# A row tile turned through DRAM is scaled and split one attention stage later, and the attention stream starts two slots sooner

## The chip, the cores and the metric

One core of one Trainium2 chip runs the whole program. TensorE (PE) does the matrix products and has a row of its own for loading weights (PEld); VectorE (DVE), ScalarE (ACT) and GpSimd (POOL) do the element-wise work; SyncE (SP) issues nearly all DMA transfers. The metric is device microseconds (us) from one launch, lower is better.

## What is computed

Three layers follow each other, in float32.

```python
# 1. gated linear attention: B 4, H 8, S 768, D 48
for t in range(S):
    state = alpha[:, :, t, :, None] * state + einsum('bhd,bhe->bhde', k[:, :, t], v[:, :, t])
    y[:, :, t] = einsum('bhd,bhde->bhe', q[:, :, t], state)
x = y.transpose(0, 2, 1, 3).reshape(B * S, H * D)      # 3072 tokens x 384
# 2. RMS norm and gated feed-forward layer, 384 -> 1536 -> 384
xn = x / sqrt(mean(x * x, -1) + 1e-6) * rms_g
x = (silu(xn @ w_gate) * (xn @ w_val)) @ w_out
# 3. eight experts, each token goes to the one with the highest logit
out[mask_e] = gate_w * sigmoid(x @ w_output_gate)[e] * (relu(x[mask_e] @ w1[e]) @ w2[e])
```

## The kernel before, in words

The 3,072 tokens are 24 tiles of 128 tokens. Three tiles form a group of 384 tokens, and the feed-forward layer runs over eight groups. A group has 12 chunks j of 128 hidden columns, and each chunk takes three **slots** of TensorE: gate(j) (nine matmuls into ps_g), val(j) (nine into ps_v) and out(j-1) (nine into ps_o, 400 columns). So a group has 36 slots. Each product is split into a high and a low part in a 32-bit form for matmuls (xh and xl for the input, hh and hl for the hidden values), hence the nine matmuls of 3 x 3. Between the slots, ACT makes tt = silu(ps_g) (L647), DVE multiplies it by ps_v (L666), ACT rounds it to hh (L669) and DVE subtracts to give hl (L675). The out slot reads hh and hl.

The attention of later tiles is woven into these slots. Every tile has five **stages** (`moved`, for tiles 9 to 23): scores (s_), a second stage, output and state together (yd_), keys (keys_) and rows (rows_). A stage runs behind the slot whose number satisfies the test in the last lines of the code below, in which `LEADG` says how many slots ahead of the even spread the stream stands. What the names mean:

- ps_y (L467, L471) is the attention output of a tile in PSUM, with P the masked scores (L443), wide a copy of the state for the next tile (L439) and ps_st (L492) the state update.
- ACT squares ps_y and sums it into ss (L477). POOL turns ss into 1/rms in two operations (L478, L479). ACT writes the normalised rows xn (L480). There is one xn buffer.
- `turn_x`, in rows_: DVE turns xn in 32 x 32 blocks into P's space (L512), four DMAs write it to DRAM as mid_x (L517), and one DMA reads it back, transposed, into xn (L518).
- `put_x`: ACT scales xn by rms_g in three pieces (L526), copies it to xh (L527), and DVE subtracts to give xl (L528). xh and xl are the input of a later group.
- `turn_k`, in keys_: DVE turns the keys of the next tile through the buffer Z (L556), four DMAs write mid_k (L561), one reads it back as kn. Z has one buffer. The next tile's scan (L318) writes Z again, behind a memset of one element by POOL (L408), and both have to wait until the mid_k writes have read Z.

The kernel goes through a tile scheduler that orders each engine's instructions by its own estimate of readiness, unless an instruction is held in source order by `keep_in_program_order`. That, and the stage table, set the order around the change.

Of the kernel before, what the change touches and what calls it, by code (L numbers as in the profile page):

```python
# [12 lines left out]
AF = mybir.ActivationFunctionType  # L13
ALU = mybir.AluOpType
# [5 lines left out]
CFG = {  # L20
    'START': 'a0 r0 a1 w6 c q0 k0 k1 r1 q1 w0 s0 s0 a2 y0 s1 r2 c q2 y0 s1 k2 w0 y1 w4 x0 y1 x1 s2 s2 y2 y2 x2 n1 n0 c n2 l l x2 d1 w3 d1 d0 w2 c x0 d2 d2 x1 w1 d0',
    'LOADS': 'a0 q0 a1 k0 q1 k1 a2 v0 w g k2 v1 q2 w v2 w w r w w w w w',
    'SEATS': (3, 5, 4, 6, 1, 1, 0, 5, 0, 2, 4, 4, 5, 0, 3, 2, 6, 1, 4, 4, 4, 2, 2, 1, 6, 3, 0, 6, 6, 4),
# [17 lines left out]
    'TS': 3,  # L41
    'RA': 7,
    'RB': 9,
    'LEADG': 11,
    'NAT': 5,
    'XO': 2,
    'MT': 6,
# [9 lines left out]
def gla_glu_moe_kernel(  # L57
# [16 lines left out]
    nc = tc.nc  # L74
# [5 lines left out]
    NTILE = NT // P  # L80
# [3 lines left out]
    KF = DFF // P  # L84
    E, _, F2 = w1.shape
    KF2 = F2 // P
    GT = 3
# [57 lines left out]
    gT = const.tile([P, KD], F32, name="gT")  # L145
# [30 lines left out]
    def f(x):  # L176
        return x.bitcast(F32)
# [240 lines left out]
    def stages(t):  # L418
# [6 lines left out]
        g, ti = divmod(t, GT)  # L425
# [77 lines left out]
        def group():  # L503
            if ti == 0:
                xT[g] = (act.tile([P, KD, G], F32R, tag="xh", name="xh"),
                         act.tile([P, KD, G], F32R, tag="xl", name="xl"))
# [13 lines left out]
        def put_x():  # L520
            group()
            xh, xl = xT[g]
            xf = Pt["xn"].rearrange("p (a b) -> p a b", a=KD)
            sl = slice(ti * P, ti * P + P)
            for kc in range(KD):
                nc.scalar.activation(xf[:, kc, :], xf[:, kc, :], AF.Copy, scale=gT[:, kc:kc + 1])  # L526
            nc.scalar.activation(xh[:, :, sl], xf, AF.Copy)  # L527
            nc.vector.tensor_tensor(out=xl[:, :, sl], in0=xf, in1=f(xh[:, :, sl]), op=ALU.subtract)  # L528
        moves[t] = (turn_x, put_x)

        def xtr():
# [22 lines left out]
    def turn_k(t):  # L554
        Z, kT = spare[t], pre[t][2]
        nc.vector.transpose(out=flat(Z).rearrange("a (c p d) -> a p c d", c=TW, p=NP),  # L556
                            in_=kT.rearrange("a p (j c) -> a p c j", c=TW))
        mid = dram.tile([P, H * 64], F32, tag="mid_k", name="mid_k", bufs=2)
        dst = mid.rearrange("(j c) (p a d) -> a j (c p) d", c=TW, p=NP, a=TW)
        for a in range(TW):  # L560
            nc.sync.dma_start(dst[a], flat(Z)[32 * a:32 * a + 32].rearrange("j (n d) -> j n d", d=32))  # L561
        kn = att.tile([P, H, 64], F32, tag="kn", name="kn")
        nc.sync.dma_start(flat(kn), mid)
        kq[t] = kn
# [259 lines left out]
    def prep_step():  # L824
        if prep:
            prep.pop(0)()

    def slot(s, n):

        g, j0, _ = runs[s]  # L830
        j, what = j0 + n // 3, n % 3
        if what == 0:
            have(3 * j + 1, 0)
            return m_gate(g, j)
        if what == 1:
            have(3 * j + 2, 0)
            return m_val(g, j)
        m_low(g, j)
        if j > j0:
            have(3 * j, j)  # L840
            m_out(s, j - 1)
        elif s:
            have(3 * runs[s - 1][2], runs[s - 1][2])
            m_out(s - 1, runs[s - 1][2] - 1)
            return lambda: m_evac(s - 1)

    NST = 5
# [65 lines left out]
    laid = []  # L913

    def moved(t):
        s_, k_, y_, d_, _ = stages(t)

        def second():
            if t == DT:
                k_()  # L920
            return laid.pop() if laid else None

        def yd_():
            posts = [y_(), d_()]

            def post():
                for p in posts:
                    if p:
                        p()
            return post  # L930

        def keys_():
            while prep:
                prep_step()
            if t + 1 < NTILE and place_of[t + 1][1] < NCH - 1:
                turn_k(t + 1)

        def rows_():
            moves[t][0]()
            laid.append(moves[t][1])  # L940
        return s_, second, yd_, keys_, rows_

    def rest():
        yield lambda: None
        yield lambda: laid.pop()

# [5 lines left out]
    done = 0  # L952
    GS = GT * NST

    def stage():
        nonlocal done, nprep
        if done % NST == 0:
            while prep:
                prep_step()
            if nprep < NTILE and done != GS - NST:  # L960
                prep.extend(prework(nprep))
                nprep += 1
        done += 1
        return next(att_stream)()
# [50 lines left out]
    def tiny(name, shape, dt=F32):  # L1015
        return xp.tile(shape, dt, name=name)
# [10 lines left out]
    def pick_first():  # L1027
        key = keys()
        km = tiny("km", [P, 1, 1])
        nc.vector.tensor_reduce(out=km, in_=key, op=ALU.max, axis=AX.X)  # L1030
        nc.vector.tensor_tensor(out=lead1, in0=key, in1=km.to_broadcast([P, 1, E]), op=ALU.is_equal)
        nc.vector.tensor_tensor(out=key, in0=lead1, in1=io8, op=ALU.mult)
        nc.vector.tensor_reduce(out=km, in_=key, op=ALU.add, axis=AX.X)
        nc.vector.tensor_tensor(out=adr[:, 0:1, :], in0=kadr, in1=km.to_broadcast([P, 1, 3]), op=ALU.mult)
        addresses(0)
# [23 lines left out]
    def load_w1(p, i):  # L1059
        n = F2 // 4  # L1060
        s = slice(i * n, i * n + n)
        st = act.tile([P, KD, n], F32, tag="stg", name="st1", bufs=4)
        nc.sync.dma_start(st, w1.rearrange("e k n -> (e k) n")[bass.ds(places[p][1], DM), s]
                          .rearrange("(kc p) n -> p kc n", p=P))

        def go():
            w1h, w1l = we[p][0:2]
            for ins in (nc.scalar.activation(w1h[:, :, s], st, AF.Copy),
                        nc.vector.tensor_tensor(out=w1l[:, :, s], in0=st, in1=f(w1h[:, :, s]), op=ALU.subtract)):
                if p == 1 and i < 4:  # L1070
                    tc.keep_in_program_order(ins)
        return go
# [102 lines left out]
    for g in range(2, NG):  # L1175
        last = g == NG - 1
        strict[0] = g + 2 >= CFG['STRICT'] and not last
        if last:
            psA.release()
            att.release()  # L1180
            xp = tc.alloc_tile_pool(name="xp", bufs=1, side="right", reuse_waits="tile")
            psE = tc.alloc_tile_pool(name="psE", bufs=1, space=PSUM)
            psR[:] = [psE, "tr"]
            w1a = [xp.tile([P, KD, F2], F32R, name=f"w1a{i}") for i in range(2)]
            x2[0] = [xp.tile([P, KD, HALF], F32R, name=f"x2a{i}") for i in range(2)]
            we[0] = [*w1a, None, None]
            lead1 = tiny("lead1", [P, 1, E])
            adr = tiny("adr", [P, E, 3], I32)
            er0 = xp.tile([P, 2, RW], F32, name="er0")
            todo = []  # L1190
        for n in range(3 * KF):
            post = slot(g + 2, n)
            if post:
                post()
            if done < (NTILE - GT) * NST + 2 and ((g - 1) * 3 * KF + n + 1 + CFG['LEADG']) * GT >= (done + 1 - GT * NST) * 3 * KF / NST:
                post = stage()
                if post:
                    post()
            prep_step()
            if g == 2 and n in (1, 3):  # L1200
                (route_a, route_b)[n // 2](0)
            if n == CFG['RA']:
                route_a(g - 1)
            if n == CFG['RB']:
                route_b(g - 1)
            if last:
                if n == 9:
                    pick_first()
                if n in (10, 12, 14, 16):
                    todo.append(load_w1(0, (n - 10) // 2))  # L1210
                if n in (18, 20, 22, 24):
                    todo.pop(0)()
                if n == 24:
                    load_rows(0, er0)
                if n >= 28 and n < 28 + 3:
                    prep_rows(0, n - 28)
                if n in (25, 27, 29, 31):
                    todo.append(load_w2(0, (n - 25) // 2))
# [254 lines left out]
```

## Time and profile before

| | |
|---|---|
| median of 3 runs | 863.0 us (862.89 to 867.31) |
| the profiled execution | 866.33 us, span 864.5 us |
| mean granted TensorE clock | 0.990 |
| PE, PEld busy | 835.1 us, 794.0 us |
| DVE, ACT, POOL busy | 513.5, 315.9, 147.3 us |

The span is the time from the first to the last instruction of the core in the profiled execution. That execution is one of its own beside the three timed runs. A busy share is a mean over the whole span. The stretch from about 200 to 550 us is where the turned tiles 9 to 23 pass.

### The profile page before, as it was taken

The page shows a single profiled execution, that of the slowest core. Times are in us where ns is not written, and L with a number is a line of the kernel's source. Part 1 is how long each engine was busy: PE and PEld are TensorE (multiplying, and loading weights), DVE is VectorE, ACT ScalarE, POOL GpSimd, SP SyncE. Part 2 cuts the span into 40 slices and gives each one's busy share as a digit, 9 for nine tenths or more (in the row PEclk, how much of TensorE's full clock was granted, in tenths as well). Part 3 has the DMA queues.
Part 4 walks back from the last instruction along what each step waited for, and adds up shares of the span by engine and source line. Part 5 has one row for each costly group of instructions (what it writes and reads, how often), then busy time and mean ns, then how long its engine had stood idle before and what let it go on. Part 6 is the DMA issues. An engine that isn't in the chain of part 4 may idle for free.

```text
span 864.5 us, 15986 instructions
## 1 busy us (share of the span) xinstructions
PE 835.1 (97%) x6111; PEld 794.0 (92%) x6111; DVE 513.5 (59%) x1136; ACT 315.9 (37%) x695; POOL 147.3 (17%) x204
## 2 busy tenths in 40 slices
PE   7999999999899999999999999999999999999996
PEld 6899999999799889898989989999988999999996
DVE  6899998697667756656666753244453442453331
ACT  1646544332323333322322332234234343453431
POOL 2100000002100010010020010013033243343341
PEclk8999999999999999999999999999999999999999
DMA  9956566755544342244454211032055164266421
GB/s 192 181 156 158 164 138 171 208 140 122 134 96 89 77 117 66 68 106 97 93 130 94 52 38 27 11 98 95 1 192 195 59 215 138 66 201 192 153 69 35
DMA packets 168990, 100.12 MB, mean 116 GB/s; under 512 B 100811, under 2 KB 162764, under 8 KB 168912
## 3 DMA queue, kind: packets, MB, share of 16 engines
q1 hardware_dynamic: 164448, 89.61, 41.7%
q0 software_dynamic: 4464, 9.48, 3.2%
q8 instruction: 48, 0.79, 0.4%
q14 instruction: 30, 0.25, 0.1%
HBM read 77.68 MB, written 21.64 MB: 115 GB/s over the span
## 4 chain that ended last, share of the span: by engine, by line
PE 57%; DMA 14%; DVE 12%; issue 6%; SPq 5%; ACT 4%; POOL 2%; POOLq 0%; DVEq 0%; ACTq 0%
PE ps_o L689 12%; PE ps_v L655 11%; PE ps_g L655 10%; PE ps_b L1155 9%; PE ps_h L655 8%; DMA xn<-mid_x 3%; DMA mid_x<-P 3%; DMA st<-in_moe_w_dram 3%; SPq L517 2%; SPq L561 2%; PE ps_s L433 2%; PE ps_y L471 2%; DMA er<-bucket 1%; DMA out_dram<-ob,ix 1%; ACT xn L526 1%
## 5 line engine op out<-in xcount | busy, mean ns | idle before, releaser
L669 ACT ACTIVATE hh<-tt 128x384 fp32r<-128x384 f32 x96 | 50.1, 522 | 142.4 <-DVE tt L666 139.7
L666 DVE TENSOR_TENSOR tt<-tt,ps_v 128x384 f32<-128x384 f32 x96 | 52.4, 545 | 71.3 <-PE ps_v L655 62.0
L675 DVE TENSOR_TENSOR hl<-tt,hh 128x384 fp32r<-128x384 f32 x96 | 54.3, 566 | 43.4 <-ACT hh L669 42.5
L1140 DVE SCALAR_TENSOR_TENSOR h<-ps_h,h 128x256 fp32r<-128x256 f32 (+6 forms) x72 | 37.9, 531 | 58.1 <-ACT h L1139 55.4
L655 PE MATMUL ps_v<-xh,wvh 128*128 128x384 f32 x192 | 67.4, 351 | 4.8 <-DVE tt L666 3.2
L689 PE MATMUL ps_o<-woh,hh 128*128 128x400 f32 x192 | 66.2, 353 | 5.6 <-ACT hh L669 5.6
L1155 PE MATMUL ps_b<-w2a,h 128*128 128x384 f32 (+2 forms) x336 | 66.6, 338 | 1.3 <-ACT h L1139 1.3
L655 PE MATMUL ps_g<-xh,wgh 128*128 128x384 f32 x192 | 67.2, 350 | 0.0
L689 PE MATMUL ps_o<-wol,hh 128*128 128x400 f32 x192 | 67.0, 349 | 0.0
L1155 PE MATMUL ps_b<-w2b,h 128*114 128x384 f32 (+3 forms) x336 | 65.5, 338 | 1.0 <-ACT h L1139 0.8
L655 PE MATMUL ps_g<-xh,wgl 128*128 128x384 f32 x192 | 65.0, 338 | 0.1
L655 PE MATMUL ps_g<-xl,wgh 128*128 128x384 f32 x192 | 64.9, 338 | 0.0
L655 PE MATMUL ps_v<-xh,wvl 128*128 128x384 f32 x192 | 64.8, 338 | 0.0
L689 PE MATMUL ps_o<-woh,hl 128*128 128x400 f32 x192 | 64.7, 350 | 0.0
L655 PE MATMUL ps_v<-xl,wvh 128*128 128x384 f32 x192 | 64.7, 337 | 0.0
L647 ACT ACTIVATE tt<-ps_g 128x384 f32<-128x384 f32 x96 | 46.6, 486 | 46.4 <-PE ps_g L655 40.3
L1155 PEld LDWEIGHTS ps_b<-w2b,h 128*114 128x114 f32 (+3 forms) x336 | 57.3, 175 | 3.6 <-ACT h L1139 1.5
L1155 PEld LDWEIGHTS ps_b<-w2a,h 128*128 128x128 f32 (+2 forms) x336 | 57.8, 181 | 2.3 <-ACT h L1139 1.6
L655 PE MATMUL ps_h<-x,w1b 128*128 128x456 f32 (+3 forms) x288 | 58.7, 344 | 0.0
L1139 ACT ACTIVATE h<-ps_h 128x256 fp32r<-128x256 f32 (+6 forms) x72 | 33.2, 467 | 62.0 <-PE ps_h L655 56.8
L478 POOL TENSOR_SCALAR ss<-ss 128x1 f32<-128x1 f32 x24 | 7.9, 330 | 279.7 <-ACT xn L477 274.8
L655 PE MATMUL ps_h<-x,w1a 128*128 128x256 f32 (+3 forms) x288 | 53.6, 328 | 0.0
(289 smaller groups left out, 1963.4 us busy)
## 6 DMA issues: line engine op xcount, KB each, us to landing
st<-in_moe_w_dram SPq DMA_DIRECT2D x64, 384.0 KB
bucket<-zero SPq DMA_DIRECT2D x8, 772.0 KB
stg<-in_moe_w_gate_dram SPq DMA_DIRECT2D x12, 384.0 KB
stg<-in_moe_w_val_dram SPq DMA_DIRECT2D x12, 384.0 KB
stg<-in_moe_w_out_dram SPq DMA_DIRECT2D x12, 384.0 KB
v<-in_v_dram SPq DMA_DIRECT2D x23, 192.0 KB
blk_a<-in_alpha_dram SPq DMA_DIRECT2D x34, 96.0 KB
blk_k<-in_k_dram SPq DMA_DIRECT2D x34, 96.0 KB
```

What stands on the lines that cost most here:

```text
L433: seq(nc.tensor.matmul(ps[hh][:, p, :], lhsT=kT[r, p, :], rhs=qT[r, p, :], start=True, stop=True))
L471: seq(nc.tensor.matmul(ps[u, h * D:h * D + D], lhsT=Pt[h % 2][:, h // 2, u], rhs=vt[t][:, h, :], start=first, stop=True, skip_group_check= ...
L517: nc.sync.dma_start(dst[c], xb[32 * c:32 * c + 32].rearrange("d (n i) -> d n i", i=32))
L647: nc.scalar.activation(tt, ps, AF.Silu)
L655: seq(nc.tensor.matmul(ps, lhsT=a_[:, kc, :], rhs=b_[:, kc, :], start=(n == 0), stop=(n == 3 * KD - 1)))
L666: nc.vector.tensor_tensor(out=tt, in0=tt, in1=ps, op=ALU.mult)
L669: nc.scalar.activation(hh, tt, AF.Copy)
L675: nc.vector.tensor_tensor(out=hl, in0=tt, in1=f(hh), op=ALU.subtract)
L689: seq(nc.tensor.matmul(obank[s][i], lhsT=a_[:, sl], rhs=weight(b_, j), start=(j == j0 and n == 0), stop=(j == j1 - 1 and n == 2)))
L1139: nc.scalar.activation(hh[:, 0, :], ps, AF.Relu)
L1140: nc.vector.scalar_tensor_tensor(out=hh[:, 1, :], in0=ps, scalar=0.0, in1=f(hh[:, 0, :]), op0=ALU.max, op1=ALU.subtract)
L1155: ins = nc.tensor.matmul(ob2[u][i][0:r], lhsT=hh[:, a_, sl], rhs=we[p][b_][:, j, :], start=(j == 0 and m == 0), stop=(j == KF2 - 1 and m = ...
```

## The change

`put_x` of tile t ran in the second stage of tile t+1. Now it runs in the third stage (yd_) of tile t+1, as the first of that stage's follow-up work, ahead of that tile's own squares and sums. Its ACT and DVE instructions are held in source order. `LEADG` goes from 11 to 13, so each stage of the stream comes two slots sooner, and one empty stage is added at the end for the last tile.

```diff
@@ -41,7 +41,7 @@
     'TS': 3,
     'RA': 7,
     'RB': 9,
-    'LEADG': 11,
+    'LEADG': 13,
     'NAT': 5,
     'XO': 2,
     'MT': 6,
@@ -523,9 +523,11 @@
             xf = Pt["xn"].rearrange("p (a b) -> p a b", a=KD)
             sl = slice(ti * P, ti * P + P)
             for kc in range(KD):
-                nc.scalar.activation(xf[:, kc, :], xf[:, kc, :], AF.Copy, scale=gT[:, kc:kc + 1])
-            nc.scalar.activation(xh[:, :, sl], xf, AF.Copy)
-            nc.vector.tensor_tensor(out=xl[:, :, sl], in0=xf, in1=f(xh[:, :, sl]), op=ALU.subtract)
+                tc.keep_in_program_order(nc.scalar.activation(xf[:, kc, :], xf[:, kc, :], AF.Copy,
+                                                              scale=gT[:, kc:kc + 1]))
+            tc.keep_in_program_order(nc.scalar.activation(xh[:, :, sl], xf, AF.Copy))
+            tc.keep_in_program_order(nc.vector.tensor_tensor(out=xl[:, :, sl], in0=xf, in1=f(xh[:, :, sl]),
+                                                             op=ALU.subtract))
         moves[t] = (turn_x, put_x)
 
         def xtr():
@@ -918,10 +920,10 @@
         def second():
             if t == DT:
                 k_()
-            return laid.pop() if laid else None
 
         def yd_():
-            posts = [y_(), d_()]
+            posts = laid + [y_(), d_()]
+            laid[:] = []
 
             def post():
                 for p in posts:
@@ -941,6 +943,7 @@
         return s_, second, yd_, keys_, rows_
 
     def rest():
+        yield lambda: None
         yield lambda: None
         yield lambda: laid.pop()
 
@@ -1192,7 +1195,7 @@
             post = slot(g + 2, n)
             if post:
                 post()
-            if done < (NTILE - GT) * NST + 2 and ((g - 1) * 3 * KF + n + 1 + CFG['LEADG']) * GT >= (done + 1 - GT * NST) * 3 * KF / NST:
+            if done < (NTILE - GT) * NST + 3 and ((g - 1) * 3 * KF + n + 1 + CFG['LEADG']) * GT >= (done + 1 - GT * NST) * 3 * KF / NST:
                 post = stage()
                 if post:
                     post()
```

The instruction streams of three engines show what this does to the order. The first place is GpSimd, at tiles 11 and 12. `Z_...` is the buffer of the key turn, `ss_...` the sum of squares of a tile. Before:

```order
L478 TENSOR_SCALAR ss_3152<-ss_3152 128x1 [waits Activation_49]
L479 TENSOR_TENSOR ss_3152<-ss_3152,mhalf_80 128x1 [waits Pool_49]
L408 MEMSET Z_3261 128x1 [waits DMAHW6_49,DMAHW5_49,DMAHW7_49,DMAHW0_49,DVE_49]
L478 TENSOR_SCALAR ss_3406<-ss_3406 128x1 [waits Activation_49]
L479 TENSOR_TENSOR ss_3406<-ss_3406,mhalf_80 128x1 [waits Pool_49]
L408 MEMSET Z_3519 128x1 [waits DMAHW6_49,DMAHW5_49,DMAHW7_49,DMAHW4_49,DVE_49]
```

After:

```order
L408 MEMSET Z_3239 128x1 [waits DMAHW6_49,DMAHW5_49,DMAHW7_49,DMAHW0_49,DVE_49]
L478 TENSOR_SCALAR ss_3128<-ss_3128 128x1 [waits Activation_49]
L479 TENSOR_TENSOR ss_3128<-ss_3128,mhalf_80 128x1 [waits Pool_49]
L408 MEMSET Z_3493 128x1 [waits DMAHW6_49,DMAHW5_49,DMAHW7_49,DMAHW4_49,DVE_49]
L478 TENSOR_SCALAR ss_3382<-ss_3382 128x1 [waits Activation_49]
L479 TENSOR_TENSOR ss_3382<-ss_3382,mhalf_80 128x1 [waits Pool_49]
```

The memset of Z, which waits for the four mid_k writes (the DMAHW names), stood behind the two operations on ss and now stands ahead of them. The same holds for tiles 11, 12, 13, 17, 18, 20 and 21, and in tile 19 the memset stands between the two.

The second place is ScalarE, around the put of one tile and the attention output of the next. Before:

```order
L669 ACTIVATE hh<-tt 128x384
L647 ACTIVATE tt<-ps_g 128x384
L669 ACTIVATE hh<-tt 128x384
L439 ACTIVATE wide_125<-state_123 48x4x48 x2
L477 ACTIVATE xn,ss<-ps_y 128x384
L480 ACTIVATE xn<-ps_y,ss 128x384
L647 ACTIVATE tt<-ps_g 128x384
L669 ACTIVATE hh<-tt 128x384
L647 ACTIVATE tt<-ps_g 128x384
L526 ACTIVATE xn<-xn,gT 128x128 x3
L705 ACTIVATE R<-ps_o 128x400
L669 ACTIVATE hh<-tt 128x384
```

After:

```order
L649 ACTIVATE tt<-ps_g 128x384
L671 ACTIVATE hh<-tt 128x384
L649 ACTIVATE tt<-ps_g 128x384
L526 ACTIVATE xn<-xn,gT 128x128 x3
L439 ACTIVATE wide_125<-state_123 48x4x48 x2
L528 ACTIVATE xh<-xn 128x3x128
L477 ACTIVATE xn,ss<-ps_y 128x384
L480 ACTIVATE xn<-ps_y,ss 128x384
L671 ACTIVATE hh<-tt 128x384
```

The three scalings and the copy to xh stood two tt and one hh behind the normalisation (L477, L480) of a tile. Now they stand ahead of the normalisation of the next tile, with the copies to wide between them. L477 now also waits for xl (L529 of the changed kernel), which reads the xn buffer that L477 writes.

On TensorE the stage yd_ moves with `LEADG`: in the steady groups the row of ps_y and ps_st stood behind out and ahead of gate, and now stands behind gate(J) and ahead of val(J). The rows_ stage of a tile and the put were five slots apart, and are seven to eight apart now.

The third place is SyncE's queue at tile 9, the first that is turned. Before:

```order
L263 DMA blk_q<-in_q_dram 32x4x192
L263 DMA blk_q<-in_q_dram 32x4x160
L517 DMA mid_x<-P_2511 384x1x32 x4
L263 DMA blk_q<-in_q_dram 32x4x192
L263 DMA blk_q<-in_q_dram 32x4x160
L561 DMA mid_k<-Z 512x1x32 x2
L518 DMA xn<-mid_x 128x384
L561 DMA mid_k<-Z 512x1x32
```

After:

```order
L263 DMA blk_q<-in_q_dram 32x4x192
L263 DMA blk_q<-in_q_dram 32x4x160
L263 DMA blk_q<-in_q_dram 32x4x192
L263 DMA blk_q<-in_q_dram 32x4x160
L517 DMA mid_x<-P_2511 384x1x32 x4
L563 DMA mid_k<-Z 512x1x32 x3
L518 DMA xn<-mid_x 128x384
```

Two more loads of blk_q now stand ahead of the four mid_x writes, and three writes of mid_k stand ahead of the read back into xn.

## Rows read from the trace of the kernel before

**Rows 1.** Profile page, busy us of each engine, share of the span, instructions.

```profile
PE 835.1 (97%) x6111; PEld 794.0 (92%) x6111; DVE 513.5 (59%) x1136; ACT 315.9 (37%) x695; POOL 147.3 (17%) x204
```

**Rows 2.** Profile page, chain that ended last, share of the span by line.

```profile
PE ps_o L689 12%; PE ps_v L655 11%; PE ps_g L655 10%; PE ps_b L1155 9%; PE ps_h L655 8%; DMA xn<-mid_x 3%; DMA mid_x<-P 3%; DMA st<-in_moe_w_dram 3%; SPq L517 2%; SPq L561 2%; PE ps_s L433 2%; PE ps_y L471 2%; DMA er<-bucket 1%; DMA out_dram<-ob,ix 1%; ACT xn L526 1%
```

**Rows 3.** Waits of ACT, 200 to 550 us: total us, times, longest.

```profile
ACT xn L526 <- DMA xn<-mid_x: 74.2, 15, 8.5
```

**Rows 4.** Waits of PE, 200 to 550 us, same columns.

```profile
PE ps_o L689 <- ACT hh L669: 6.0, 5, 3.5
PE ps_v L655 <- DVE tt L666: 4.6, 5, 1.5
```

**Rows 5.** Waits of PE's weight loads, 200 to 550 us, same columns.

```profile
PEld ps_v L655 <- DVE tt L666: 9.1, 10, 1.9
PEld ps_o L689 <- ACT hh L669: 8.5, 8, 3.8
PEld ps_o L689 <- DVE hl L675: 2.3, 7, 0.4
```

**Rows 6.** Timeline of one tile: start us, duration, engine, line; idle before, releaser.

```profile
293.70 1.13 DVE L556 STREAM_TRANSPOSE Z<-kT 128x512 f32<-128x512 f32 x1
...
294.50 0.73 ACT L439 ACTIVATE wide<-state 48x192 f32<-48x192 f32 x2 [1.31 <-PE ps_y L467]
...
295.42 0.49 ACT L477 ACTIVATE xn<-ps_y 128x384 f32<-128x384 f32 x1 [0.18 <-PE ps_y L471]
...
296.21 0.68 POOL L478 TENSOR_SCALAR ss<-ss 128x1 f32<-128x1 f32 x1 [22.07 <-ACT xn L477]
...
297.56 0.58 ACT L480 ACTIVATE xn<-ps_y,ss 128x384 f32<-128x384 f32 x1 [1.43 <-POOL ss L479]
...
298.17 0.86 DVE L512 STREAM_TRANSPOSE P<-xn 128x384 f32<-128x384 f32 x1 [0.20 <-ACT xn L480]
...
300.28 1.22 DVE L318 TENSOR_TENSOR_SCAN Z<-aT,begin 128x511 f32<-128x511 f32 x1 [0.75 <-DMA mid_k<-Z]
...
300.29 0.10 POOL L408 MEMSET Z<- 128x1 f32 x1 [2.77 <-DMA mid_k<-Z]
...
309.78 0.99 ACT L526 ACTIVATE xn<-xn,gT 128x128 f32<-128x128 f32 x3 [6.60 <-DMA xn<-mid_x]
...
311.21 0.56 DVE L675 TENSOR_TENSOR hl<-tt,hh 128x384 fp32r<-128x384 f32 x1 [6.33 <-ACT hh L669]
...
311.23 0.45 PE L689 MATMUL ps_o<-woh,hh 128*128 128x400 f32 x1 [0.95 <-ACT hh L669]
...
312.11 0.35 PE L689 MATMUL ps_o<-woh,hh 128*128 128x400 f32 x1
```

**Rows 7.** Timeline of the tile before it: VectorE's turn, GpSimd's memset.

```profile
268.54 1.12 DVE L556 STREAM_TRANSPOSE Z<-kT 128x512 f32<-128x512 f32 x1
...
274.05 0.10 POOL L408 MEMSET Z<- 128x1 f32 x1 [1.68 <-DVE en L315]
```

**Rows 8.** Chain of waits, and a window: us, busy by engine, PEclk, DMA.

```profile
236.65 3.30 PE ps_o L689 x9
...
237.00:238.00 1.00, 1.00 (x4) 0.85 (x4) 1.00 (x3) 0.00 (x0) 0.00 (x0) 0.50 0.00 0
```

**Rows 9.** Timeline at the second turned tile: TensorE, VectorE and SyncE.

```profile
212.73 0.34 PE L655 MATMUL ps_v<-xh,wvh 128*128 128x384 f32 x1
...
214.30 0.35 PE L689 MATMUL ps_o<-woh,hh 128*128 128x400 f32 x1
...
216.06 0.88 PE L467 MATMUL ps_y<-wide,qT 128*64 128x96 f32 x16
...
218.25 0.44 PE L655 MATMUL ps_g<-xh,wgh 128*128 128x384 f32 x1
...
215.25 1.29 DVE L443 TENSOR_TENSOR P<-ps_s,mask 128x512 f32<-128x512 f32 x2 [2.79 <-DMA mid_x<-P]
...
212.68 1.25 SPq L263 DMA_DIRECT2D blk_q<-in_q_dram  x2
```


## Prediction

> **What bounds the kernel now.** I read the page first: PE is busy 835.1 of 864.5 us [rows 1], so about 29 us without a matmul is all there is to win unless work is taken away, and this change takes none away. The chain that ended last comes next [rows 2]. Most of it is matmuls, but the way of a row tile through DRAM stands on it by name: the write mid_x 3%, the read back 3%, its issue 2%. In the waits of ACT over the stretch of the turned tiles, the first scaling of `put_x` (L526) waits 74.2 us for that read, 15 times, one for each turned tile [rows 3]. ACT is not the bound, so that is not yet a loss. What is queued behind L526 on ACT decides, and that is hh, which the out matmuls need. So the waits of PE and of its weight loads come last: matmuls wait 6.0 us for hh and 4.6 us for tt [rows 4], weight loads 8.5, 9.1 and (for hl) 2.3 us [rows 5]. One tile shows how: xn is turned at 298.17, L526 begins at 309.78 after 6.60 us of idle ACT, hl comes behind it at 311.21 and the out matmuls begin at 311.23 after 0.95 us without one [rows 6]. A wait of 6.6 us on ACT thus became about one on PE: TensorE had a slot of work in hand.
>
> **Term 1, the wait removed.** From the turn to L526 it is 11.6 us [rows 6]. After the change the put stands one stage later, behind the gate slot of the next tile. Tiles follow each other by 25.2 us here (268.54 to 293.70 [rows 6, 7]). Call E the end of gate(J), the slot behind which the stage runs. By the sum of term 2 the turn then begins at about E+6, and ACT comes to the put at the next E plus 0.5, 25.2 + 0.5 - 6 = 19.7 us after the turn. That leaves 8 us over the 11.6, so the transfer is hidden in the steady part, and the stalls that L526 causes go. How much of PE's time is that? By matmul rows 10.6 us (6.0 + 4.6), by weight loads 19.9 us (8.5 + 9.1 + 2.3). The one stall that I can follow lies between: 0.95 us ahead of the first matmul, and then the first three steps take 312.11 - 311.23 = 0.88 us where three steps at the pace of rows 9 (nine matmuls in 214.30 - 212.73 = 1.57 us) take 0.52 us, so 0.36 us more, 1.31 in all [rows 6, 9]. Scaled by 1.31/0.95 the matmul sum gives 14.6 us; I take 15.5, with 10.6 and 19.9 as its bounds.
>
> The Trainium skill, in Perfetto Trace Analysis (section Identifying the Most-Contended Engine), says that matmul busy time is a poor measure because pipelined matmuls look smaller in the trace, and that the busy share of weight loads is a better one. By that alone this term would be 19.9 us and the time some 4 us lower; the stall of 1.31 us above, between the two rows, bears it out in direction.
>
> **Term 2, the clock.** The longest stall, 3.5 us [rows 4], was followed by out matmuls at a granted clock of 0.50, the lower of the two levels (1.2 of 2.4 GHz): nine took 3.30 us [rows 8], against 1.57 for nine of 384 columns, 1.64 for their 400. That is some 1.5 us, which goes with the stall. Sum of what goes: 17.0 us.
>
> **Term 3, what takes its place in the steady tiles.** Work after E, from durations of rows. PE: ps_y and ps_st 2.19 us (218.25 - 216.06), val 1.57, out 1.76 (216.06 - 214.30), gate 1.57, val 1.57, and the third matmul of the next out, the first that reads hl(J), 0.35 more [rows 9]. PE needs hl(J) at E+9.0. The way to hl(J): ACT does tt 0.5, three scalings 0.99, wide 0.73, xh 0.5; DVE does xl 0.55; ACT squares 0.49 and reads the sum 0.2 (E+4.0); POOL's two operations take 297.56 - 296.21 = 1.35; then xn 0.58, DVE's turn 0.86, the scan 1.22 and hl 0.56, which stand in this order on DVE [rows 6] (tt and xh are taken like xn, xl like hl). The sum is E+8.6, with 0.4 us to spare: xl and the waiting L477 cost nothing, as TensorE's two slots and the attention matmuls cover them, and those are used up.
>
> But in seven tiles the memset of Z now stands ahead of POOL's two operations. It waits for the mid_k writes. In the trace it stood behind them, and its wait cost POOL alone. From the turn of the keys to the memset it is 300.29 - 293.70 = 6.6 us and, as an upper bound where a DVE instruction released it, 274.05 - 268.54 = 5.5 us [rows 6, 7]. The turn of the keys begins after hl(J-1) and kT*Z, by the same count at E-0.8. POOL is then free at E+4.7 to E+5.8 and not at E+4.0. From there 1.35 + 0.58 + 0.86 + 1.22 + 0.56 = 4.6 us lead to the end of hl(J), E+9.3 to E+10.4: a stall of 0.3 to 1.4 us, queued behind it xn, the turn, the scan and hl, with PE waiting last. I take the middle, about 0.8 us seven times, with nothing for the tile where it stands between the two: 5.5 us. Bounds: 0 (the writes land by E+4, or the out matmuls find slack in the val slot) and 7 x 1.4 = 10 us.
>
> **Term 4, the start.** At the second turned tile the DVE product P waits 2.79 us for mid_x, whose DMAs read the same buffer [rows 9], and PE loses almost nothing, because ps_y stands behind out there. Now ps_y stands one slot sooner, behind val, and two more blk_q loads, 1.25 us on SP's queue [rows 9], stand ahead of the mid_x writes. P begins at about 215.25 + 1.25 = 216.5 and its first half ends 0.65 later, at 217.15; PE comes to the P part at 214.30 + 0.88 = 215.2. That is 2.0 us, and tt, hh and the squares behind it slip as well, where POOL's 1.35 us and xn 0.58 stand in the way: about 2 more. I take 4.0, between 0 (SP's queue has room) and 6. All other edits cost nothing: the same instructions run as before, held order included, and the last tile's put comes a slot later than before with five slots to its group.
>
> **The sum** against the profiled execution's own 866.33 us: -17.0 + 5.5 + 4.0 = -7.5, 858.8 us. That execution was 3.3 us above the median of 863.0. On the median the forecast is 855.5, and I say **855 us**.
>
> **Rivals.**
> A, the forecast: term 3 at 0.3 to 1.1 a tile, 851 to 859 us. Chance 0.45.
> B, the memset costs PE nothing. mid_k lands by E+4.7 and the gap is eaten by slack: -17 + 4 or less, 846 to 850 us. For it: the shorter of the two distances [rows 7], and the third matmul is only the latest need. Against: the longer [rows 6]. Chance 0.22.
> C, the new wait eats the gain. The put, the normalisation, the turn and the scan form one line ahead of hl in all 15 tiles, with 0.4 us to spare; if ACT, POOL and DVE hand over later than the sum says (each hand-over 0.2 us, as the turn's own wait of 0.20 in rows 6), five of them use it up and add 0.6 us in each of 15 tiles, 9 us on top of terms 3 and 4: -17 + 18, 864 us. Chance 0.20.
> D, slower. The mid_k writes land 2 us later than in rows 6, because the stream runs closer to the blk loads. The stall is then 1.4 + 2 = 3.4 us in eight tiles, 27 us, and each is as long as the one that was followed by the granted clock of 0.50 [rows 4, 8], at 1.5 us each: 12 us. -17 + 4 + 27 + 12 gives 889 us at full effect, 872 to 876 if half of the tiles see it. It decides from a stall of 17/8 = 2.1 us per tile. Against it: no landing of before is that late. Chance 0.09. The Trainium skill's DMA: Bandwidth & Descriptors (section Latency and other measured facts) gives 0.2 us for an access to the chip's memory on average and 2 us at high load, which would be such a delay; no stretch of this trace shows it.
> E, the change does not do what it says. ACT's 74.2 us were nearly hidden from PE, and the order of hh and tt alone moved: within 2 us of 863. Chance 0.04.
>
> **How the numbers follow.** The time is that of A. The range takes B whole and C nearly: 846 to 866. A measurement of this kernel can hardly tell 0.5%, 858.7 to 867.3, from no change. Faster: B and nearly nine tenths of A, 0.61. Within: the rest of A, most of C, E: 0.28. Slower: D and a little of C, 0.11.
>
> **What would show it.** The waits of ACT no longer hold L526 with more than a few us in all (term 1; if not, E). PE's waits for hh and tt lose most of their 10.6 us, and no window near 237 us has a granted clock of 0.50. POOL's memset waits for mid_k ahead of ss, and L480 waits for POOL 2 us and more in seven tiles (term 3); ps_v and ps_o then wait for tt, hh or hl in those tiles alone. At about 215 us ps_y waits for P (term 4). I am wrong if mid_k lands much earlier or later than 6 us after its turn, if PE waits in tiles where POOL isn't held (C), or if the stream's earlier start moves stalls into the groups before 200 us.

## The result and the profile after

The changed kernel takes 851.07 us, the median of 4 runs (850.14 to 854.04), against 865.06 us for the kernel before (862.89 to 867.31, 4 runs). The ratio is 0.984, with an interval of 0.980 to 0.989. The medians lie 14.0 us apart, where 8 were forecast; the kernel before has one run more here than ahead of the prediction, and its four lie in two pairs, near 863 and near 867 us. In a second set of five runs the changed kernel took 852.26 us against 863.82 (ratio 0.986, 0.984 to 0.988). The forecast of 855 lay on the right side and was too small a gain.

The profiled execution took 850.14 us with a span of 848.4 us. Its page, busy time by engine and then the chain that ended last by line, answers to [rows 1, 2]:

```profile
PE 825.8 (97%) x6111; PEld 790.3 (93%) x6111; DVE 515.1 (61%) x1136; ACT 317.5 (37%) x695; POOL 142.8 (17%) x204
...
PE ps_o L691 16%; PE ps_v L657 15%; PE ps_g L657 14%; PE ps_b L1158 8%; PE ps_h L657 7%; DMA st<-in_moe_w_dram 5%; PE ps_s L433 2%; DMA mid_k<-Z 1%; PE ps_y L471 1%; DMA out_dram<-ob,ix 1%; PE ps_y L467 1%; DMA er<-bucket 1%; DVE Z L318 1%; SPq L563 1%; DVE P L443 1%
```

The transfers of mid_x have left the chain; mid_k<-Z has come onto it, with 1%. PE's busy time fell by 9 us for the same 6,111 matmuls; matmuls at the lower clock, as in [rows 8], stand in it as longer ones.

The waits of ACT over 200 to 550 us (total, times, longest) answer to [rows 3]:

```profile
ACT tt L649 <- PE ps_g L657: 83.5, 46, 3.4
ACT xn L480 <- POOL ss L479: 27.8, 15, 3.6
ACT xn L477 <- DVE xl L529: 8.6, 13, 0.7
```

The wait of L526 for the read of mid_x, 74.2 us before, is gone altogether. What idles ACT now is the gate product, which is work of PE. The waits of PE itself, against [rows 4]:

```profile
PE ps_o L691 <- DVE hl L677: 3.0, 4, 1.3
PE ps_y L471 <- DVE P L443: 1.8, 1, 1.8
PE ps_g L657 <- ACT tt L649: 1.4, 1, 1.4
```

and of its weight loads, against [rows 5]:

```profile
PEld ps_o L691 <- DVE hl L677: 4.9, 6, 1.6
...
PEld ps_y L471 <- DVE P L443: 2.0, 1, 2.0
...
PEld ps_g L657 <- ACT tt L649: 1.7, 1, 1.7
```

So hh and tt, which PE waited for before, are on time, and the three waits that are left are hl in the tiles, P and tt at the start. A tile in the timeline, against [rows 6] (start, duration, engine, operation, idle before and releaser):

```profile
284.22 0.39 ACT L526 ACTIVATE xn<-xn,gT 128x128 f32<-128x128 f32 x1
...
287.05 0.49 ACT L477 ACTIVATE xn<-ps_y 128x384 f32<-128x384 f32 x1 [0.68 <-DVE xl L529]
...
289.29 0.10 POOL L408 MEMSET Z<- 128x1 f32 x1 [22.80 <-DMA mid_k<-Z]
...
289.48 0.19 POOL L478 TENSOR_SCALAR ss<-ss 128x1 f32<-128x1 f32 x1
...
290.33 0.58 ACT L480 ACTIVATE xn<-ps_y,ss 128x384 f32<-128x384 f32 x1 [2.70 <-POOL ss L479]
...
290.95 0.88 DVE L512 STREAM_TRANSPOSE P<-xn 128x384 f32<-128x384 f32 x1 [1.53 <-ACT xn L480]
...
291.88 1.22 DVE L318 TENSOR_TENSOR_SCAN Z<-aT,begin 128x511 f32<-128x511 f32 x1
...
293.02 0.53 DVE L677 TENSOR_TENSOR hl<-tt,hh 128x384 fp32r<-128x384 f32 x1
...
293.61 0.45 PE L691 MATMUL ps_o<-woh,hl 128*128 128x400 f32 x1 [0.47 <-DVE hl L677]
```

The first scaling comes at 284.22 with no wait. The squares wait 0.68 us for xl and end at about 287.5. GpSimd takes up ss only at 289.48, behind the memset that has waited for mid_k, some 1.9 us later. From there ss, xn, the turn, the scan and hl follow each other, and the third out matmul waits 0.47 us for hl. At the second turned tile (VectorE, SyncE, TensorE, weight loads; against [rows 9]), first the turn of the tile ahead of it and its mid_x writes in the kernel before:

```profile
207.99 0.85 DVE L512 STREAM_TRANSPOSE P<-xn 128x384 f32<-128x384 f32 x1
...
209.53 3.10 SPq L517 DMA_DIRECT2D mid_x<-P  x4
```

and then in the changed kernel:

```profile
206.31 0.86 DVE L512 STREAM_TRANSPOSE P<-xn 128x384 f32<-128x384 f32 x1
...
207.41 3.52 SPq L517 DMA_DIRECT2D mid_x<-P  x4
...
211.40 0.88 PE L467 MATMUL ps_y<-wide,qT 128*64 128x96 f32 x16
...
213.31 0.69 DVE L443 TENSOR_TENSOR P<-ps_s,mask 128x512 f32<-128x512 f32 x1 [2.50 <-DMA mid_x<-P]
...
214.06 0.26 PE L471 MATMUL ps_y<-v,P 128*64 128x48 f32 x2 [1.78 <-DVE P L443]
...
224.04 0.19 PEld L657 LDWEIGHTS ps_g<-xh,wgh 128*128 128x128 f32 x1 [1.70 <-ACT tt L649]
```

P waits for mid_x as before, but PE now waits 1.78 us for P, and some 10 us later the weight loads of the gate product wait 1.70 us for tt.

To compare kernels without noise from elsewhere I use one distance in each trace, called **the stream** below: from the last transposition of the tiles that TensorE turns (ps_x, whose place no edit here moves) to the first expert matmul (ps_h). Instructions of a tile in the trace, with first and last start. Before:

```profile
L539 PE MATMUL ps_x<-ident,xn x24: 271/272/421, 22.9 to 190.8; 128*128 128x128 f32 x24
...
L655 PE MATMUL ps_h<-x2a,w1a x72: 276/283/367, 611.1 to 632.4; 128*128 128x256 f32 x72
```

After:

```profile
L541 PE MATMUL ps_x<-ident,xn x24: 271/273/330, 19.6 to 187.8; 128*128 128x128 f32 x24
...
L657 PE MATMUL ps_h<-x2a,w1a x72: 277/283/368, 596.7 to 618.0; 128*128 128x256 f32 x72
```

Before, the stream is 611.1 - 190.8 = 420.3 us, after 596.7 - 187.8 = 408.9: 11.4 us less. The spans differ by 16.1. The other 4.7 us lie outside: 1.7 us in the expert phase behind, and 3.0 us ahead of the stream, where both kernels run the same instructions. There the profiled execution of before had a stretch at the lower clock (window 10 to 20 us: busy time by engine, granted clock, DMA share, GB/s),

```profile
10.00:20.00 10.00, 9.74 (x77) 8.35 (x78) 9.01 (x21) 1.10 (x3) 0.31 (x3) 0.72 1.26 245
```

which that of after had not:

```profile
10.00:20.00 10.00, 9.63 (x105) 7.92 (x103) 9.96 (x23) 1.60 (x4) 1.15 (x3) 1.00 1.26 245
```

The traces of four more runs below have it too (changed, again; lead 13 alone; memset on VectorE; lead 13 later), and the others don't, edits or not. A pair of profiled executions alone would have overrated the change. In the second set of runs the medians differ by 863.82 - 852.26 = 11.6 us, as the streams do.

The table adds two sums over the whole stream of each trace: what weight loads wait for other engines and for DMAs (time that the trace puts down to "issue" is left out), and how long the granted clock stood at 0.50.

| kernel | median us | stream us | weight loads wait, us | at clock 0.50, us | ACT waits for the read, us |
|---|---|---|---|---|---|
| before | 865.06 | 420.3 | 20.8 | 3.4 | 74.2 |
| changed | 851.07 | 408.9 | 9.6 | 0 | 0 |
| changed, again | 852.26 | 409.4 | 10.1 | 0 | 0 |
| put later and held, lead 11 | 845.79 | 402.3 | 3.0 | 0 | 5.0 |
| lead 13 alone | 864.60 | 424.1 | 20.3 | 10.2 | 63.6 |
| changed, not held | 867.07 | 425.2 | 22.1 | 10.2 | 61.7 |
| hold alone | 845.00 | 401.4 | 1.9 | 0 | 5.1 |
| changed, memset on VectorE | 850.60 | 407.6 | 8.1 | 0 | 0 |
| changed, extra transfer | 853.49 | 410.3 | 9.6 | 3.4 | 0.2 |
| changed, lead 13 later | 848.90 | 404.8 | 5.9 | 0 | 5.0 |
| before, extra transfer | 888.31 | 437.9 | 38.5 | 3.4 | 71.8 |
| hold alone, extra transfer | 848.74 | 403.8 | 4.7 | 0 | 8.5 |
| changed, lead later, memset on VectorE | 847.32 | 404.5 | 5.3 | 0 | 5.1 |

Medians are to be compared with the kernel before of their own set: 864.84 us for the four kernels from "put later and held, lead 11" to "hold alone", 862.90 for the last three, 863.82 for "changed, again" and the other three.

At 0.50 the nine out matmuls took 3.30 us [rows 8] where 1.76 is usual [rows 9], so about half of such a stretch is lost. The stream less the waits of weight loads and less half of the time at 0.50 comes to 397.7 to 399.5 us in all thirteen traces. These two sums account for the differences of up to 36.5 us between the streams to within 2 us. With the waits of the matmuls in place of the weight loads, 400.8 to 407.3 us are left.

### The profile page after: what moved, and what is told of

Its sections match the earlier page's. It is cut to its first block, busy times and chain, and to the rows that moved or that the text cites. A ratio compares the mean times of both kernels' runs of the same rounds, so it can differ in the third digit from the quotient of the medians.

```text
span 848.4 us, 16017 instructions
## 1 busy us (share of the span) xinstructions
PE 825.8 (97%) x6111; PEld 790.3 (93%) x6111; DVE 515.1 (61%) x1136; ACT 317.5 (37%) x695; POOL 142.8 (17%) x204
## 4 chain that ended last, share of the span: by engine, by line
PE 68%; DVE 11%; DMA 9%; issue 5%; ACT 2%; SPq 2%; POOL 2%; POOLq 0%; DVEq 0%; ACTq 0%
PE ps_o L691 16%; PE ps_v L657 15%; PE ps_g L657 14%; PE ps_b L1158 8%; PE ps_h L657 7%; DMA st<-in_moe_w_dram 5%; PE ps_s L433 2%; DMA mid_k<-Z 1%; PE ps_y L471 1%; DMA out_dram<-ob,ix 1%; PE ps_y L467 1%; DMA er<-bucket 1%; DVE Z L318 1%; SPq L563 1%; DVE P L443 1%
## 5 line engine op out<-in xcount | busy, mean ns | idle before, releaser
L657 PEld LDWEIGHTS ps_h<-x,w1b 128*128 128x128 f32 x288 | 50.3, 188 | 1.2 <-DVE h L1143 0.2
```

The costliest lines, as they stand in the source:

```text
L657: seq(nc.tensor.matmul(ps, lhsT=a_[:, kc, :], rhs=b_[:, kc, :], start=(n == 0), stop=(n == 3 * KD - 1)))
```

## The experiments

**The three parts of the change, one by one.** The change moves the put a stage later, holds it in source order, and starts the stream two slots sooner. My theory was that the wait of the scalings for the read paid; the rival, that the earlier stream did.

The put later and held, the lead as before:

```diff
-    'LEADG': 13,
+    'LEADG': 11,
```

> The put moved and held as in the changed kernel, but the stream's lead left at 11 slots. Theory W (the wait of the first scaling on ACT for the read of mid_x is what paid, and the later place of the put alone takes it away): ACT's waits of L526 for the read fall from 74.2 us to under 10, and the memset of Z stands behind the two operations on ss again, so the 4.9 us that weight loads waited for hl in the changed kernel and the 3.7 us at its first turned tiles need not come: 843 to 852 us against 863 before. Rival S (the earlier stream paid): 859 to 864 us.

Measured: 845.79 us (842.82 to 849.21), ratio 0.979 (0.976 to 0.983). The wait that is left on ACT is that of one tile, the first:

```profile
ACT xn L526 <- DMA xn<-mid_x: 5.0, 1, 5.0
```

So it is faster than the changed kernel, and the earlier stream doesn't pay but costs: 6.6 us in the stream (408.9 less 402.3). The lead alone, in the kernel before:

```diff
-    'LEADG': 11,
+    'LEADG': 13,
```

> The kernel before with a lead of 13 slots and nothing else changed. In its order the three scalings stand two tt behind ps_y's normalisation, nearer than before. Theory W: L526 goes on waiting for the read of mid_x, 70 us or more in all, so the time is 860 to 872 us. Rival S (the earlier stream paid): 850 to 855 us, as in the changed kernel.

Measured: 864.60 us, ratio 1.000 (0.998 to 1.003). ACT waits nearly as much as before, if less than the 70 us that I asked:

```profile
ACT xn L526 <- DMA xn<-mid_x: 63.6, 15, 7.0
```

and PE's loss has moved from hh to the gate product, which waits until ACT has emptied its buffer:

```profile
PE ps_g L655 <- ACT tt L647: 11.8, 8, 4.1
```

The stream is 3.8 us longer than before. That isn't more waiting: weight loads wait 20.3 us in it, against 20.8. But the granted clock stands at 0.50 in three stretches, at about 238, 313 and 456 us, each right behind a wait of weight loads for tt of 2.8 to 4.5 us, where before there was one such stretch. The window from 313 to 314 us (as in [rows 8], granted clock 0.50):

```profile
313.00:314.00 1.00, 1.00 (x5) 1.00 (x5) 1.00 (x3) 0.09 (x1) 0.00 (x0) 0.50 0.02 8
```

Rival S falls. Now the changed kernel without its hold:

```diff
-                tc.keep_in_program_order(nc.scalar.activation(xf[:, kc, :], xf[:, kc, :], AF.Copy,
-                                                              scale=gT[:, kc:kc + 1]))
-            tc.keep_in_program_order(nc.scalar.activation(xh[:, :, sl], xf, AF.Copy))
-            tc.keep_in_program_order(nc.vector.tensor_tensor(out=xl[:, :, sl], in0=xf, in1=f(xh[:, :, sl]),
-                                                             op=ALU.subtract))
+                nc.scalar.activation(xf[:, kc, :], xf[:, kc, :], AF.Copy, scale=gT[:, kc:kc + 1])
+            nc.scalar.activation(xh[:, :, sl], xf, AF.Copy)
+            nc.vector.tensor_tensor(out=xl[:, :, sl], in0=xf, in1=f(xh[:, :, sl]), op=ALU.subtract)
```

> The changed kernel without the hold in source order for the put's ACT and DVE instructions. The scheduler then places the scalings one tt behind the normalisation of their own tile, although the put is written a stage later. Theory W: the wait of L526 is back, 70 us or more on ACT, and the time is 860 to 872 us. Rival H (the later stage pays, the hold is an extra): 850 to 856 us.

Measured: 867.07 us, ratio 1.004 (1.002 to 1.006), no better than before. The wait on ACT is back, again a little under the 70 us that I asked:

```profile
ACT xn L526 <- DMA xn<-mid_x: 61.7, 15, 6.8
```

and with it PE's waits:

```profile
PE ps_g L655 <- ACT tt L647: 8.0, 7, 2.0
PE ps_v L655 <- DVE tt L666: 4.6, 4, 2.7
```

Written a stage later, but free to move, the scalings go back to a place one tt behind their own tile's normalisation (seen in the tile at about 300 us), as in the kernel with the lead alone; the streams of these two differ by 1.1 us. So the later stage does nothing without the hold. Does the hold do it without the later stage? In the kernel before:

```diff
             for kc in range(KD):
-                nc.scalar.activation(xf[:, kc, :], xf[:, kc, :], AF.Copy, scale=gT[:, kc:kc + 1])
-            nc.scalar.activation(xh[:, :, sl], xf, AF.Copy)
-            nc.vector.tensor_tensor(out=xl[:, :, sl], in0=xf, in1=f(xh[:, :, sl]), op=ALU.subtract)
+                tc.keep_in_program_order(nc.scalar.activation(xf[:, kc, :], xf[:, kc, :], AF.Copy,
+                                                              scale=gT[:, kc:kc + 1]))
+            tc.keep_in_program_order(nc.scalar.activation(xh[:, :, sl], xf, AF.Copy))
+            tc.keep_in_program_order(nc.vector.tensor_tensor(out=xl[:, :, sl], in0=xf, in1=f(xh[:, :, sl]),
+                                                             op=ALU.subtract))
```

> The kernel before with the put in its old stage and a lead of 11, but its ACT and DVE instructions held in source order: the scalings then stand three tt and three hh behind the normalisation, against two and one. Theory W: three chunks of about 5 us lie between, more than the 11.6 us from the turn to the data, so L526 waits under 10 us in all and the time is 844 to 852 us. Rival H (the later stage is what pays): L526 still waits 30 us or more and the time is 858 to 864 us.

Measured: 845.00 us (842.48 to 846.79), ratio 0.977 (0.974 to 0.980), the fastest of all. Its timeline for one tile, ACT's normalisation, VectorE's turn, ACT's first scaling:

```profile
286.01 0.58 ACT L480 ACTIVATE xn<-ps_y,ss 128x384 f32<-128x384 f32 x1 [1.37 <-POOL ss L479]
...
286.62 0.87 DVE L512 STREAM_TRANSPOSE P<-xn 128x384 f32<-128x384 f32 x1 [0.20 <-ACT xn L480]
...
300.14 0.39 ACT L526 ACTIVATE xn<-xn,gT 128x128 f32<-128x128 f32 x1
```

The scaling starts 13.5 us behind the turn with no wait; in the kernel before, ACT came to it at 303.18 (309.78 less 6.60 us of idle time, [rows 6]), 5.0 us behind it. Nearly all waits of PE's weight loads go. The longest that are left:

```profile
PEld ps_v L657 <- DVE tt L668: 0.7, 2, 0.6
...
PEld ps_g L657 <- ACT tt L649: 0.6, 1, 0.6
```

The stream is 18.9 us shorter than before, against 11.4 in the changed kernel. The hold alone is the gain; the other two edits together give 7.5 us of it back. Of these, 0.9 us go with the later place of the put (402.3 less 401.4, both with a lead of 11) and 6.6 with the lead. The hold with a lead of 13 and the put in its old stage was not run, so whether the later place is of use with that lead is not shown.

**Where the 7.5 us go.** Weight loads wait 9.6 us in the changed kernel's stream and 1.9 in that of the hold alone. The difference of 7.7 us lies mostly in the three waits shown above: 4.9 us for hl, 2.0 for P, 1.7 for the gate buffer. The second set ran beside the changed kernel itself.

> The changed kernel itself, again, beside the next three kernels on the same chip: 850 to 852 us, some 5 to 6 us more than the kernel with the hold alone (845.0 us).

Measured: 852.26 us (849.47 to 853.95), stream 409.4 us. First, the memset that makes GpSimd wait:

```diff
-            nc.gpsimd.memset(Z[:, NP - 1, P - 1:P], 1.0)
+            nc.vector.memset(Z[:, NP - 1, P - 1:P], 1.0)
             pre[t] = (after_scan(Z, aT), qT, kT)
```

> The changed kernel with the one-element memset of Z done by VectorE ahead of its own scan, so that GpSimd waits for no mid_k write ahead of the two operations on ss. Theory M (that memset is what holds hl back in the tiles where weight loads wait 4.9 us for it): the waits of ps_o for hl fall under 1 us and the time by 3 to 5 us, to 846 to 848 us. Rival N (the line put, squares, ss, turn, scan is too long by itself, whoever does the memset, since the scan waits for mid_k as well): within 1 us of the changed kernel.

Measured: 850.60 us (848.93 to 853.25), 1.7 us less in the median and 1.8 in the stream: less than theory M asked, more than N. The intervals of the two ratios (0.984 to 0.988, and 0.982 to 0.986) overlap. The weight loads' waits say the same:

```profile
PEld ps_o L691 <- DVE hl L677: 2.0, 3, 0.7
...
PEld ps_v L657 <- DVE tt L668: 1.9, 2, 1.2
```

Hl fell from 5.0 to 2.0, but tt rose from 0.5 to 1.9. The reason is on VectorE, which now waits for the mid_k writes with tt behind the memset in its queue:

```profile
DVE Z L408 <- DMA mid_k<-Z: 13.5, 9, 2.4
```

So taking the memset off GpSimd took 3.0 us from the wait for hl and gave 1.4 back to tt, since the wait for mid_k now stood in VectorE's queue. It doesn't show that the scan has to wait for the write whoever does the memset: VectorE's waits in the changed kernel hold no wait of the scan (L318) for mid_k at all, where the kernel before has 7.2 us of them over 200 to 550 us. With a lead of 13, a kernel in which nothing ahead of ss or tt waits for mid_k was not run, so what the 2.0 us that stay come from is open.

Second, the start of the stream:

```diff
-... + n + 1 + CFG['LEADG']) * GT >= ...
+... + n + 1 + (11 if g == 2 and n < 20 else CFG['LEADG'])) * GT >= ...
```

> The changed kernel with a lead of 11 slots up to slot 20 of the first group of the stream and of 13 from there on. Theory P (the two waits at the first turned tiles, 2.0 us for P and 1.7 us for tt, come from the earlier stage there): both go, and the time falls by 3 to 4 us, to 846.5 to 848 us. Rival Q: the wait moves to the slot where the lead jumps, and the time stays within 1 us of the changed kernel.

Measured: 848.90 us (847.04 to 853.41), 3.4 us less than the changed kernel beside it, and 4.6 in the stream. The wait for P at the first turned tiles is gone, that for tt is down from 1.7 to 1.0 us, and no new one stands at the jump. Theory P holds in the main: tt still waits, and the time is 0.9 us above what it gave. Both edits together, the memset on VectorE and the later lead:

> The changed kernel with the lead of 11 slots in the first group up to slot 20 and with VectorE's memset of Z, both costs of the earlier stream taken away that could be: 848.9 us less about 1.5, 846.5 to 848 us, still not under the 845.0 us of the kernel with the hold alone. If the two edits do not add, 849 to 851 us.

Measured: 847.32 us (845.39 to 848.65), stream 404.5 us, the rest of the gap to 401.4 us not closed. They do not add up in the stream (404.8 with the first alone). Weight loads there still wait 2.3 us for tt, 1.3 for hl and 1.1 for the gate buffer, 4.7 us, of which the kernel with the hold alone has 1.3; the 3.4 between them are about the 3.1 us that remain.

**How far the transfer is hidden.** Three kernels got one more transfer on the way:

```diff
+            far = dram.tile([P, KD * P], F32, tag="far_x", name="far_x", bufs=2)
+            nc.sync.dma_start(far, mid)
-            nc.sync.dma_start(xn, mid)
+            nc.sync.dma_start(xn, far)
```

In the changed kernel:

> The changed kernel with one more transfer, from mid_x to a second DRAM tile, ahead of the read back into xn: about 5 us more between turn and data. By the theory W the data lands about 9 us before the scalings need it in the steady tiles, so it costs 0 to 2 us: 850 to 853 us. If the transfer is only just hidden, ACT waits up to 5 us more in 15 tiles, and the time is 865 us or more.

Measured: 853.49 us (852.06 to 855.40), 1.2 us more than beside it; in the stream 0.9, in which there is also a stretch of 3.4 us at a granted clock of 0.50, behind the wait for P. VectorE's turn and ACT's first scaling of a tile lie 17.1 us apart, and the scaling shows no wait:

```profile
292.41 0.88 DVE L512 STREAM_TRANSPOSE P<-xn 128x384 f32<-128x384 f32 x1 [1.97 <-ACT xn L480]
...
309.48 0.39 ACT L528 ACTIVATE xn<-xn,gT 128x128 f32<-128x128 f32 x1
```

In the kernel before:

> The kernel before with one more transfer, from mid_x to a second DRAM tile, ahead of the read back into xn, some 5 us more between turn and data. Theory W (the wait of the first scaling is exposed on PE beyond some 5.5 us of work in hand): ACT waits 120 us or more for the read in all, each wait of about 11 us costs PE 3 to 6 us, 15 times, and the granted clock falls in some of them: 890 to 940 us. If the read were hidden behind matmuls before, the time would stay within 5 us of 863.

Measured: 888.31 us (879.57 to 894.71), ratio 1.032 (1.028 to 1.036): 25 us slower by the medians (23 without the longest of the four runs), just short of what I expected, and not for the reason that I gave. The trace is of the shortest run, 879.57 us, with a stream 17.6 us longer than before. ACT waits no longer than without the transfer,

```profile
ACT xn L528 <- DMA xn<-far_x: 71.8, 15, 7.7
```

since the scalings now stand one hh later in ACT's order (behind tt, hh, tt, hh in the tile at 298 us, where they stood behind tt, hh, tt), and since the transfer adds less than the 5 us that I took: L526 (L528 here) begins 10.0 to 14.2 us after the turn, against 7.2 to 11.6 before, 2.3 us more on average. But at the new place tt and the next silu are what stands behind them, and PE loses far more:

```profile
PE ps_v L657 <- DVE tt L668: 15.9, 13, 2.6
PE ps_g L657 <- ACT tt L649: 12.2, 10, 2.6
```

28.1 us by these two rows against 10.6 us before [rows 4], for about the same wait on ACT (71.8 and 74.2 us). In the kernel with the hold alone:

> The kernel with the hold alone (put in its old stage, lead 11) and the same extra transfer. Its scalings stand 13.3 us behind the turn (263.83 to 277.16 us in its trace), so data that takes about 16 us comes some 3 us late: L526 waits 25 to 50 us in all. By theory W, waits of about 3 us are shorter than the work that PE has in hand, and the time stays at 845 to 849 us. If any wait on ACT there counted, it would be 860 us or more. The changed kernel with the same transfer took 853.5 us with no wait, so this also tells what the later stage buys.

Measured: 848.74 us (846.25 to 850.41), as expected, but the waits are shorter than I worked out:

```profile
ACT xn L528 <- DMA xn<-far_x: 8.5, 2, 7.4
```

Two tiles wait, most of it in the first. The hold gives 10.6 to 14.8 us from turn to scaling, which is nearly enough even for the longer way of 10.0 to 14.2 us. The changed kernel gives 13.0 to 18.5 us, a spare that no kernel here needed but for that first tile. With some 2 us more on the way and not 5, both runs are a milder trial than was meant.

## Why the prediction was right, and where it was off

**Term 1 and 2, the wait and the clock: right in mechanism, under by 2 us, and put down to the wrong edit.** I had 17.0 us; the hold alone measured 18.9. The 19.9 us of weight-load waits [rows 5] fell to 1.3 us there, 18.6 us less, and the matmul waits only from 10.6 us to 0.6: the weight-load rows had the size, and the scaling of one stall to 14.6 us came out low. The Trainium skill, in Perfetto Trace Analysis (section Identifying the Most-Contended Engine), holds the busy share of weight loads to be a better measure than that of matmuls, since pipelined matmuls look smaller in a trace. It speaks of busy time and not of waits; the waits here go the same way. The clock was sized well: the stretch at 0.50 lasted 3.4 us, of which half is 1.7, where I had 1.5, and no window of the stream in the changed kernel's trace has a granted clock of 0.50.

What failed is the step "the put stands one stage later, ... so the transfer is hidden". I read the new distance from the instruction streams and took it for the work of the stage. I had 19.7 us from turn to scaling; the trace has 16.7 to 18.5 us from the third turned tile on, enough all the same, and it is the hold that brings it. (The turn at E+6 in that step is the sum of term 3, not of term 2, and the 11.6 us from turn to data are the longest of the fifteen; the others are 7.2 to 11.5.) I also wrote that the held order costs nothing and gave it no share in the gain; without it the gain is zero (867.07 us).

**Term 3, GpSimd's memset: size right, and the wait where I put it.** I had 5.5 us over the tiles; weight loads waited 4.9 us for hl, in tiles 11, 12, 13, 17, 18 and 20, six of the seven in which the memset stands ahead of ss. GpSimd was released at 289.29 in the tile shown, 5.6 us behind the end of its gate slot at about 283.7, inside the E+4.7 to E+5.8 that I gave. That excludes rival C, which has the wait in all 15 tiles. That the memset alone is the cause is shown only in part: with it on VectorE the wait for hl fell by 3.0 us, and the stream by 1.8, for VectorE then waited for the same write. With a lead of 11 the memset stands behind ss in these tiles and no wait for hl is left, so term 3 belongs to the lead, as term 4 does.

**Term 4, the start: size right, in part by luck.** I had 4.0 us, 2.0 for P and about 2 for tt; the trace shows 1.97 on the weight loads and 1.70, and undoing the lead there gives 3.4 us in the median and 4.6 in the stream. But the two blk_q loads that I charged with 1.25 us delayed nothing. The mid_x writes are issued 1.1 us after the turn begins (207.41 - 206.31), against 1.5 before, and P begins 7.0 us after it (213.31 - 206.31), against 7.3 (215.25 - 207.99). What moved is ps_y: it begins 5.1 us after the turn (211.40 - 206.31), where it was 8.1 (216.06 - 207.99), 3.0 us sooner against P and not the one slot of 1.8 that I took. A delay that wasn't there and a shift that was too small made the right sum. And of the 1.70 us for tt, 0.6 stay in the kernel with the hold alone, where the stream starts as before.

**The sum.** Forecast -17.0 + 9.5 = -7.5 us. In the stream the runs give -18.9 + 7.5 = -11.4 us. Each side was off by 2 us, and both errors went the same way. The 851.07 us lie at the lower end of A's 851 to 859, nearer to B's 850 than to the 855 that I said, by a larger term 1 and not by a free memset. D did not come: the longest wait of a weight load in the stream was 2.0 us. E is excluded.

## What to carry to other kernels

A wait on an engine that isn't the bound costs what is queued behind it on that engine, so the cure is the place in the queue, and where a scheduler chooses that place by its own estimate of readiness, a later place in the source is worth nothing until the instruction is held there. When a change bundles an order, a place and a lead, try each alone: here the one that looked like a detail made the whole gain, and the two others gave 40% of it back (7.5 of 18.9 us), nearly all of it the lead. For a loss on TensorE, sum the waits of the weight loads, not those of the matmuls, and add half of the time at the lower clock: here that explained thirteen traces to within 2 us.

## What I had not expected of the hardware

The stretch at a granted clock of 0.50 from about 14 to 25 us comes and goes between executions of the same instructions and costs 3.0 us (last ps_x at 190.5 to 190.8 us with it, at 187.2 to 188.1 without). What sets it off stays open. PE runs the same instructions in both, but not at the same times: in the five traces that have it PE stood idle for 0.2 to 0.7 us at about 10 us, waiting for a read of in_k, and of the eight others only one did, for 0.2 us. GpSimd's first operation on ss took 0.68 us after 22.07 us of idle time before [rows 6] and 0.19 us after 21.98 us with the memset on VectorE:

```profile
289.97 0.19 POOL L478 TENSOR_SCALAR ss<-ss 128x1 f32<-128x1 f32 x1 [21.98 <-ACT xn L477]
```

In the trace of before alone it took 0.62 us after 2.85 us of idle time and 0.19 after 20.79. So the idle time alone doesn't set its price; what does is not settled by these runs.
